# A recurrent cross-attention block with a three-way maxout FFN: transposes moved to DMA, the state read turned round, and the first batch split by halves of heads

## The chip, the cores and the metric

The kernel runs on one core of one Trainium2 chip. The metric is the device time of one execution in microseconds, the lower the better. Three runs of the kernel before gave 189.73, 190.93 and 191.05 us, median 190.93 us. The profile is of one further execution.

## The reference

For each of 8 batches and 8 heads there are 512 tokens x and 32 states, both 64 wide. Tokens attend to states, states attend to tokens, and the 544 rows that result go, with the heads side by side as 512 columns, through a maxout FFN.

```python
B, H, S, Ns, D = 8, 8, 512, 32, 64          # n_tokens 4352, d_model 512, d_ff 768
scores = scale * x @ state^T                 # per batch and head: 512 x 32
a      = softmax(scores, over the states)
xread  = a @ state                           # 512 x 64
a2     = softmax(scale * state @ x^T, over the tokens)
sread  = a2 @ x                              # 32 x 64
y      = concat([xread, sread], rows), heads side by side      # (8*544) x 512
h      = max(max(y @ w1, y @ w2), y @ w3)    # w: 512 x 768
out    = h @ w_out                           # w_out: 768 x 512
```

Both softmaxes come from the same exponentials e = exp(scale * scores), and no maximum is subtracted in the kernel. For the token rows the kernel never forms xread: since xread @ w = a @ (state @ w), it computes G = state @ w for each batch (a row for every head and state, 256 rows by 2304 columns) and multiplies that by the transposed a.

## The kernel before, in words

TensorE (PE) does all products. In the names below, b is a batch, m one of six slices of 128 columns of d_ff, j one of four groups of 128 tokens, h a head.

- `xt_piece` transposes x of a batch on PE, 16 blocks of 128x128, into `pxt`; ScalarE (ACT) copies it out as `xT` (lines 134 and 135).
- `score_piece` makes the scores `ps` from `xT` and `bd`, the transposed states laid out block-diagonally for pairs of token groups. ACT takes the exponential `e`; VectorE (DVE) sums it (`den`) and inverts (`rden`); GpSimd (POOL), for batch 0 DVE, multiplies to `a`.
- `sread_piece` makes sread with x as the stationary and e as the moving operand, 32 matmuls of 32 columns, then 8 matmuls with a tile of ones for the denominators. DVE divides into `ats`, which holds the state rows of all batches, already transposed.
- `at_piece` transposes a on PE (8 blocks, `pat`); DVE copies it out as `aT`.
- `g_piece` makes one sixth of G: 8 small matmuls in 8 tiles of the array (4 column groups by 2 row groups) into `pg`, and an ACT copy of 128x768 (line 208).
- `maxout` makes, for one m, three products `pw` of 512 columns (w1, w2, w3), and takes the maximum: ACT copies the first out (`t`, line 222), DVE takes the two maxima (lines 223 and 224) into `ht`.
- `ffn_out` multiplies `ht` by w_out for two token groups at once into `po` (12 matmuls), ACT copies 128x1024 out (line 251), and SP starts the output DMA.

Each engine works its instructions off in the order in which the program writes them; that order is written out by hand. The loop over b runs `x_maxout(b, m)` for m = 0 to 5, and behind each m come the pieces of the next batch and the output of the batch before: after m = 0 `xt_piece`, after 1 `score_piece`, after 3 `sread_piece`, after 4 `at_piece`, after each m one `g_piece`, and after 2 and 5 (ahead of that `g_piece`) half of `ffn_out(b - 1)`. In the last batch the slots hold `s_maxout`, the maxout of the state rows. Ahead of the loop, batch 0 goes through all pieces in turn.

PSUM has eight banks: the pool "pw" is a ring of four single banks, which only `pw` uses after the start; the pool "two" is two buffers of two banks, for `pxt`, `ps`, `psr`, `pat`, `pg` and `po`. Matmuls that would reuse a buffer wait until its reader is done.

Loads: x of batch 0 in two halves on SP's queue, all states in one DMA on ACT's, and the weights (cut into two halves of d_ff) and the other x on POOL's queue, which converts to bf16 in flight.

Of the kernel before, what the change touches and what calls it, by code (L numbers as in the profile page):

```python
# [15 lines left out]
def kernel(  # L16
# [86 lines left out]
    pt = [pp.tile([128, 8, 128], BF16, tag="pw", bufs=4, name=f"pt{k}") for k in range(2)]
    for t in range(16):
        nc.tensor.transpose(pt[t // 8][:, t % 8, :], st_sb[:, t].rearrange("p c d -> p (c d)"), ident)
    nc.vector.tensor_copy(out=x_sb[0][:, 0:4].rearrange("p h j d -> p h (j d)"), in_=x_f[0])
    nc.scalar.copy(out=x_sb[0][:, 4:8].rearrange("p h j d -> p h (j d)"), in_=x_f[1])  # L109

    def bd_piece(b0, b1):
        for k in range(2):
            for c, copy in enumerate((nc.vector.tensor_copy, nc.scalar.copy)):
                r = slice(64 * c, 64 * c + 64)
                dst = bd[r, b0:b1, :, c, :].rearrange("p b h (g t) -> p (b h) g t", t=16)
                copy(out=dst[:, :, :, 8 * k:8 * k + 8],
                     in_=pt[k][r, :, 16 * b0:16 * b1].rearrange("p t (k g) -> p k g t", g=2))

    bd_piece(0, 1)


    xT, e, a, aT, G, ht = {}, {}, {}, {}, {}, {}

    def xt_piece(b):

        xT[b] = work.tile([128, H, 2, 128], BF16, tag="xT", name="xT")
        pxt = pp.tile([128, H, 2, 128], BF16, tag="two", name="pxt")
        for h in range(H):
# [197 lines left out]
```

## Time and profile before

| | us |
|---|---|
| median of three runs | 190.93 |
| the profiled execution's own time | 189.44 |
| its span, in which the rows below count | 187.6 |
| PE busy | 163.5 (87%) |
| ACT busy | 106.2 (57%) |
| DVE busy | 103.3 (55%) |
| POOL busy | 28.0 (15%) |

The profiled execution is 1.49 us shorter than the median of the runs, and 1.84 us of it lie outside the span. A busy share is an average over the whole span. The span has stages with different limits: a start in which batch 0 goes through its pieces, the loop over the batches, and an end in which only outputs are left. The rows below are read stage by stage. A row of the timeline merges neighbouring instructions of one line; its first number is the start, the second how long the group took.

### The profile page before, as it was taken

How to read it: one execution, taken by the hardware profiler on the slowest of the kernel's cores; microseconds unless marked ns; L12 is line 12 of the kernel's file. 1: busy time of each engine (PE TensorE's matmuls, PEld its weight loads, DVE VectorE, ACT ScalarE, POOL GpSimd, SP SyncE). 2: the span in 40 equal slices, each digit the busy share in tenths (PEclk: the TensorE clock that was granted, in tenths of full speed). 3: DMA queues.
4: the chain of work that ended last, by engine and by line, in shares of the span. 5: the costliest groups of instructions: out<-in, count | busy, mean ns of one | idle time of the engine just before them, and what ended most of it. 6: DMA issues, size and time to landing. Idle time of an engine off the chain costs nothing.

```text
span 187.6 us, 3845 instructions
## 1 busy us (share of the span) xinstructions
PE 163.5 (87%) x1604; PEld 84.8 (45%) x1604; DVE 103.3 (55%) x161; ACT 106.2 (57%) x151; POOL 28.0 (15%) x31
## 2 busy tenths in 40 slices
PE   0643699899999999999999999999999999999990
PEld 0632244454445444544454454445454546565530
DVE  4429325994592559255925683467447747476100
ACT  3542769469455955495549554955495544242330
POOL 8710000500500050005000500040004000000021
PEclk9999999999999999999999999999999999999998
DMA  5999990180192019110911092202020202020236
GB/s 194 265 203 203 203 165 3 6 106 3 77 151 84 31 56 165 68 54 33 182 47 77 9 193 37 103 0 112 5 112 0 115 2 112 3 112 0 112 139 197
DMA packets 15216, 17.53 MB, mean 93 GB/s; under 512 B 672, under 2 KB 12704, under 8 KB 15200
## 3 DMA queue, kind: packets, MB, share of 16 engines
q0 software_dynamic: 11360, 7.08, 27.1%
q1 hardware_dynamic: 3696, 9.70, 13.3%
q10 hardware_dynamic: 144, 0.52, 0.8%
q8 instruction: 12, 0.20, 0.4%
q14 instruction: 4, 0.03, 0.1%
HBM read 15.20 MB, written 8.91 MB: 129 GB/s over the span
## 4 chain that ended last, share of the span: by engine, by line
PE 54%; ACT 18%; DVE 16%; issue 6%; DMA 4%; SPq 0%; DVEq 0%; ACTq 0%
PE pw L218 22%; PE po L243 22%; ACT G L208 7%; PE pg L203 4%; PE pxt L130 4%; DVE rd L176 4%; ACT xT L135 4%; DVE t L223 4%; DMA xf<-in_x_dram 3%; DVE ht L224 3%; ACT xT L134 2%; ACT t L222 2%; ACT osb L251 2%; DVE ats L177 1%; DVE den L148 1%
## 5 line engine op out<-in xcount | busy, mean ns | idle before, releaser
L218 PE MATMUL pw<-aT,G 128*128 128x512 bf16 x288 | 72.0, 384 | 0.7 <-ACT t L222 0.6
L223 DVE TENSOR_TENSOR t<-t,pw 128x512 bf16<-128x512 bf16 (+1 forms) x54 | 34.9, 647 | 55.4 <-ACT t L222 52.1
L208 ACT CAST G<-pg 128x768 bf16<-128x768 f32 x48 | 38.8, 812 | 15.6 <-PE pg L203 15.5
L243 PE MATMUL po<-wout,ht 128*128 128x512 bf16 x204 | 46.5, 379 | 0.0
L218 PEld LDWEIGHTS <-G 128*128 128x128 bf16 x288 | 24.8, 98 | 32.5 <-issue 11.3
L224 DVE TENSOR_TENSOR ht<-t,pw 128x512 bf16<-128x512 bf16 (+1 forms) x54 | 35.5, 658 | 6.0 <-PE pw L218 0.5
L251 ACT COPY osb<-po 128x1024 f32<-128x1024 f32 x16 | 16.2, 1012 | 37.3 <-PE po L243 37.3
L222 ACT CAST t<-pw 128x512 bf16<-128x512 f32 (+1 forms) x54 | 31.4, 584 | 6.9 <-PE pw L218 5.4
L153 POOL TENSOR_TENSOR a<-e,rden 128x1024 bf16<-128x1024 bf16 x7 | 13.3, 1904 | 116.9 <-DVE rden L150 116.9
L243 PEld LDWEIGHTS <-ht 128*128 128x128 bf16 x204 | 19.9, 98 | 23.9
L203 PE MATMUL pg<-w,bd 64*32 64x384 bf16 x384 | 18.1, 353 | 7.2 <-DVE ats L177 6.1
L203 PEld LDWEIGHTS <-bd 64*32 64x32 bf16 x384 | 6.6, 90 | 17.3 <-issue 9.8
L134 ACT COPY xT<-pxt 128x1024 bf16<-128x1024 bf16 x8 | 8.1, 1012 | 5.0 <-PE pxt L130 5.0
L148 DVE TENSOR_REDUCE den<-e 128x32 f32<-128x1024 bf16 x8 | 9.7, 1213 | 2.0 <-ACT e L146 2.0
L130 PE MATMUL pxt<-ident,x 128*128 128x128 bf16 x128 | 9.5, 231 | 0.1
L146 ACT ACTIVATE e<-ps 128x1024 bf16<-128x1024 f32 x8 | 8.5, 1064 | 1.6 <-PE ps L141 1.6
L130 PEld LDWEIGHTS <-x 128*128 128x128 bf16 x128 | 8.5, 104 | 2.0 <-ACT x L109 0.4
L218 PE MATMUL pw<-ats,w 128*128 128x256 bf16 x72 | 9.0, 272 | 0.2 <-ACT t L222 0.2
L141 PE MATMUL ps<-bd,xT 128*128 128x64 bf16 x128 | 5.6, 199 | 3.7 <-ACT xT L135 2.3
L141 PEld LDWEIGHTS <-xT 128*128 128x128 bf16 x128 | 5.1, 101 | 6.9 <-issue 4.3
L218 PEld LDWEIGHTS <-w 128*128 128x128 bf16 x72 | 7.0, 98 | 2.4 <-issue 0.3
L176 DVE RECIPROCAL rd<-psr 128x128 f32<-128x128 f32 x8 | 7.6, 949 | 0.0
(37 smaller groups left out, 78.6 us busy)
## 6 DMA issues: line engine op xcount, KB each, us to landing
out_dram<-osb SPq DMA_DIRECT2D x15, 512.0 KB, 2.6
x<-in_x_dram POOLq DMA_DIRECT2D x7, 512.0 KB, 7.1
w<-in_moe_w_dram POOLq DMA_DIRECT2D x6, 384.0 KB, 10.6
xf<-in_x_dram SPq DMA_DIRECT2D x2, 512.0 KB, 5.9
wout<-in_moe_w_out_dram POOLq DMA_DIRECT2D x1, 768.0 KB, 18.6
stf<-in_state_dram ACTq DMA_DIRECT2D x1, 512.0 KB, 4.1
out_dram<-osb SPq DMA_DIRECT2D x2, 256.0 KB, 3.0
out_dram<-osb SPq DMA_DIRECT2D x4, 64.0 KB, 1.7
```

The costliest lines, as they stand in the source:

```text
L130: nc.tensor.transpose(pxt[:, h, jj, :], x_sb[b][:, h, 2 * jj:2 * jj + 2, :].rearrange("p j d -> p (j d)"), ident)
L134: nc.scalar.copy(out=xT[b][:, 0:4], in_=pxt[:, 0:4])
L153: mul(out=a[b].rearrange("p j h n -> p (j h) n"), in0=e[b].rearrange("p j h n -> p (j h) n"), in1=rden.rearrange("p j h -> p (j h)").unsqu ...
L176: nc.vector.reciprocal(out=rd, in_=psr[:, 128:256])
L203: nc.tensor.matmul(pg[32 * hh:32 * hh + 32, r, 0:384], bd[64 * r:64 * r + 64, b, h, r, :], w_sb[c][64 * r:64 * r + 64, hh, k * 384:(k + 1) ...
L208: nc.scalar.copy(out=G[b][:, :, u * 384:(u + 1) * 384], in_=pg[:, :, 0:384])
L218: nc.tensor.matmul(p[:, 0:n], lhs(i, m, k), rhs(k), start=(k == 0), stop=(k == nk - 1))
L222: nc.scalar.copy(out=t0[:, 0:n], in_=pw[0][:, 0:n])
L223: nc.vector.tensor_max(t1[:, 0:n], t0[:, 0:n], pw[1][:, 0:n])
L224: nc.vector.tensor_max(ht[b][:, m, :], t1[:, 0:n], pw[2][:, 0:n])
L243: nc.tensor.matmul(po[:, j - j0, :], ht[b][:, m, j * 128:(j + 1) * 128], wout_sb[:, m, :], start=(m == 0), stop=(m == NM - 1))
L251: nc.scalar.copy(out=o, in_=po)
```

## The change

The arithmetic is the same up to rounding. The parts:

- **First batch.** x of batch 0 comes in two halves by parity of the head; the states of batch 0 have a small DMA of their own (`st0`) and a tile of their own (`bd0`), the rest (`stf`, `bdr`) comes third on SP's queue. Scores, softmax and transposes of batch 0 run by halves. `x_maxout(0, m)` starts when the first sixth of G is there, and the other sixths are made in between. Batch 1 has its front part behind batch 0, with PE transposes; the loop starts at b = 1.
- **Weights** are loaded in three chunks of d_ff: one slice, two slices, three slices. G is stored by slice of d_ff, and one `g_cols` call makes one or two slices; from batch 1 on they come in pairs.
- **sread** has e as the stationary operand (32 columns wide, four column tiles of the array) and x with a block of ones behind it as the moving operand, 128 columns: the denominators come out of the same 32 matmuls. The result `sr` is not yet transposed.
- **DMA transposes** on SP's queue: `sr` into `ats` for every batch, `x` into `xT` and `a` into `aT` from batch 2 on.
- **po in single banks**: `ffn_out` works on one token group (6 matmuls, one bank of the ring "pw", an ACT copy of 128x512). `psr` uses that ring too.
- **keep_busy** puts five matmuls on zeros at the start of PE's program.

The diff, cut to its core (removed lines are left out except at the loads; they are the functions shown above):

```diff
--- before.py
+++ after.py
...
+    st0_f = data.tile([128, 2, D], F32, name="st0f")
+    nc.scalar.dma_start(out=st0_f, in_=state[0].rearrange("h n d -> (h n) d").rearrange("(t p) d -> p t d", p=128))
+    x0_f = [data.tile([128, HS, J * D], F32, name=f"x0f{g}") for g in range(2)]
+    for g in range(2):
+        nc.sync.dma_start(
+            out=x0_f[g], in_=x[0].rearrange("(s g) (p j) d -> g p s (j d)", g=2, j=J)[g])
     st_f = data.tile([128, 16, D], F32, name="stf")
-    nc.scalar.dma_start(
+    nc.sync.dma_start(
         out=st_f, in_=state.rearrange("b h n d -> (b h n) d").rearrange("(p t) d -> p t d", t=16))
-    x_f = [data.tile([128, 4, J * D], F32, name=f"xf{g}") for g in range(2)]
-    for g in range(2):
-        nc.sync.dma_start(out=x_f[g], in_=x_rows(0)[:, 4 * g:4 * g + 4, :])
+    zero = const.tile([128, 512], BF16, name="zero")
+    nc.vector.memset(zero, 0.0)
     ident = const.tile([128, 128], BF16, name="ident")
     make_identity(nc, ident)
...
+    chunks = ((0, 1), (1, 3), (3, 6))
+    w_sb = [wpool.tile([128, HS, 3, (m1 - m0) * 128], BF16, name=f"w{m0}") for m0, m1 in chunks]
     wout_sb = wpool.tile([128, NM, d_model], BF16, name="wout")
     def load_w(c):
+        m0, m1 = chunks[c]
         for i, w in enumerate((moe_w1, moe_w2, moe_w3)):
             nc.gpsimd.dma_start(
+                out=w_sb[c][:, :, i, :],
+                in_=w.rearrange("(kk p) f -> p kk f", p=128)[:, :, m0 * 128:m1 * 128])
...
     load_w(0)
     load_w(1)
+    bd0 = data.tile([128, H, 2, Ns], BF16, name="bd0")
+    nc.vector.memset(bd0, 0.0)
+    bdr = data.tile([128, B - 1, H, 2, Ns], BF16, name="bdr")
+    for b in range(B):
+        nc.vector.memset(x_sb[b][:, XW:XW + D], 1.0)
+    load_w(2)
     load_x(1)
     nc.gpsimd.dma_start(out=wout_sb, in_=moe_w_out.rearrange("(kk p) f -> p kk f", p=128))
-    ones = const.tile([128, 64], BF16, name="ones")
-    nc.vector.memset(ones, 1.0)
+    nc.gpsimd.memset(bdr, 0.0)
+    load_x(2)
...
+    def keep_busy(n):
+        p = pp.tile([128, 1024], F32, tag="two", name="idle")
+        for _ in range(n):
+            nc.tensor.matmul(p[:, 0:512], zero[:, 0:128], zero, start=True, stop=True)
...
+    def states_first():
+        st0 = data.tile([128, 2, 2, D], BF16, name="st0")
+        nc.vector.tensor_copy(out=st0, in_=st0_f.unsqueeze(2).to_broadcast((128, 2, 2, D)))
+        p = pp.tile([128, 2, 128], BF16, tag="pw", bufs=4, name="pt0")
+        for t in range(2):
+            nc.tensor.transpose(p[:, t, :], st0[:, t].rearrange("p c d -> p (c d)"), ident)
+        for c, copy in enumerate((nc.vector.tensor_copy, nc.scalar.copy)):
+            r = slice(64 * c, 64 * c + 64)
+            copy(out=bd0[r, :, c, :], in_=p[r].rearrange("p t (h n) -> p (t h) n", n=Ns))
...
+    def x_transpose_dma(b):
+        new(xT, b, [128, H, 2, 128], "xT")
+        nc.sync.dma_start_transpose(out=xT[b].rearrange("p h j t -> p (h j) t"), in_=x_sb[b][:, 0:XW])
...
+        if n == 2:
+            p = pp.tile([128, J, n, HS, Ns], F32, tag="two", name="ps")
+        else:
+            p = pp.tile([128, J, n, HS, Ns], F32, tag="pw", bufs=4, name="psh")
...
+    def a_transpose_dma(b):
+        new(aT, b, [128, J, 2, 128], "aT")
+        nc.sync.dma_start_transpose(
+            out=aT[b].rearrange("p j g t -> p (j g) t"), in_=a[b].rearrange("p j g s n -> p (j g s n)"))
+    def sread(b):
+        p = pp.tile([128, 2, 2, D], F32, tag="pw", bufs=4, name="psr")
         for j in range(J):
+            for g in range(2):
+                for s in range(HS):
+                    xj = xv[b][:, 2 * s + g, j, :]
+                    both = bass.AP(xj.tensor, xj.offset,
+                                   (xj.ap[0], (XW - ((2 * s + g) * J + j) * D, 2), (1, D)))
+                    nc.tensor.matmul(
+                        p[32 * s:32 * s + 32, g], e[b][:, j, g, s, :], both,
+                        start=(j == 0 and g == 0), stop=(j == J - 1), skip_group_check=True,
+                        tile_position=(0, 32 * s))
+        rd = work.tile([128, 2, 1], F32, tag="rd", name="rd")
+        nc.vector.reciprocal(out=rd, in_=p[:, :, 1, 0:1])
+        sr = work.tile([128, 2, D], BF16, tag="sr", name="sr")
+        nc.vector.tensor_mul(out=sr, in0=p[:, :, 0, :], in1=rd.to_broadcast((128, 2, D)))
+        nc.sync.dma_start_transpose(
+            out=ats[:, b].rearrange("p s n -> p (s n)"), in_=sr.rearrange("p g d -> p (g d)"))
+    def g_cols(b, ms):
+        for m in ms:
+            if m == 0:
+                new(G, b, [128, 2, NM * 384], "G")
+            w, f = w_cols(m)
+            p = pp.tile([128, 2, 512], F32, tag="two", name="pg")
+            for s in range(HS):
+                for g in range(2):
+                    nc.tensor.matmul(
+                        p[32 * s:32 * s + 32, g, 0:384].rearrange("p (i f) -> p i f", i=3),
+                        bd(b, 2 * s + g)[64 * g:64 * g + 64, g, :], w[64 * g:64 * g + 64, s, :, f],
+                        start=True, stop=True, tile_position=(64 * g, 32 * s))
...
+    def ffn_out(b, j, split=False):
+        if j == 0:
+            osb[b] = work.tile([128, J, d_model], F32, tag="osb", name="osb")
+        p = pp.tile([128, d_model], F32, tag="pw", bufs=4, name="po")
+        for m in range(NM):
+            nc.tensor.matmul(p, ht[b][:, m, j * 128:(j + 1) * 128], wout_sb[:, m, :],
+                             start=(m == 0), stop=(m == NM - 1))
+        o = osb[b]
+        if split:
+            nc.scalar.copy(out=o[:, j, 0:256], in_=p[:, 0:256])
+            nc.vector.tensor_copy(out=o[:, j, 256:512], in_=p[:, 256:512])
         else:
+            nc.scalar.copy(out=o[:, j, :], in_=p)
...
+        j0 = j if b == B - 1 and j >= 2 else j - 1
+        if j == 1 or j == 3 or j0 == j:
+            nc.sync.dma_start(
+                out=out[b * SP:b * SP + S, :].rearrange("(p j) f -> p j f", j=J)[:, j0:j + 1, :],
+                in_=o[:, j0:j + 1, :])
...
+    keep_busy(5)
+    states_first()
+    dve(out=xv[0].rearrange("p (s g) j d -> p g s (j d)", g=2)[:, 0], in_=x0_f[0])
+    act(out=xv[0].rearrange("p (s g) j d -> p g s (j d)", g=2)[:, 1], in_=x0_f[1])
+    x_transpose(0, 0, dve)
+    x_transpose(0, 1, dve)
+    for g in range(2):
+        scores(0, g, g + 1)
+        softmax(0, g, g + 1, nc.vector.tensor_mul)
+    g_cols(0, (0,))
+    a_transpose(0, 0, act)
+    a_transpose(0, 1, dve)
+    x_maxout(0, 0)
+    states_rest()
+    sread(0)
+    g_cols(0, (1, 2))
+    x_maxout(0, 1)
+    x_maxout(0, 2)
+    g_cols(0, (3, 4))
+    x_maxout(0, 3)
+    x_maxout(0, 4)
+    g_cols(0, (5,))
+    x_maxout(0, 5)
+    x_transpose(1, 0, act)
+    x_transpose(1, 1, dve)
+    x_transpose_dma(2)
+    scores(1, 0, 2)
+    softmax(1, 0, 2, nc.vector.tensor_mul)
+    load_x(3)
+    sread(1)
+    g_cols(1, (0, 1))
+    ffn_out(0, 0)
+    g_cols(1, (2, 3))
+    ffn_out(0, 1)
+    a_transpose(1, 0, act)
+    a_transpose(1, 1, dve)
+    g_cols(1, (4, 5))
+    pending = [(0, 2), (0, 3)]
+    for b in range(1, B):
+        n = b + 1
         slots = [[] for _ in range(NM)]
+        if n < B:
+            slots[0].append(lambda: scores(n, 0, 2))
+            slots[0].append(lambda: softmax(n, 0, 2, nc.gpsimd.tensor_mul))
+            slots[1].append(lambda: g_cols(n, (0, 1)))
+            slots[3].append(lambda: sread(n))
+            slots[3].append(lambda: a_transpose_dma(n))
+            slots[4].append(lambda: g_cols(n, (2, 3)))
+            slots[5].append(lambda: g_cols(n, (4, 5)))
+            if n + 1 < B:
+                slots[4].append(lambda: x_transpose_dma(n + 1))
+            if n + 2 < B:
+                slots[1].append(lambda: load_x(n + 2))
         else:
             for m in range(NM):
                 slots[m].append(lambda m=m: s_maxout(m))
+        for m in (1, 2, 4, 5):
+            if pending:
+                slots[m].append(lambda t=pending.pop(0): ffn_out(*t))
...
+        pending += [(b, j) for j in range(J)]
+    ffn_out(B - 1, 0)
+    ffn_out(B - 1, 1)
+    ffn_out("s", 0)
+    ffn_out("s", 1)
+    ffn_out(B - 1, 2)
+    ffn_out(B - 1, 3, split=True)
```

SP's instruction queue, the whole program before: two loads, then only outputs.

```order
L68 DMA xf_82<-in_x_dram 128x4x256
L68 DMA xf_83<-in_x_dram 128x4x256
L258 DMA out_dram<-osb 128x1024 x15
L255 DMA out_dram<-osb 32x512 x4
L258 DMA out_dram<-osb 128x512 x2
```

SP's queue now, from the output of batch 0 to the output of batch 2 (x_90 and x_91 are x of batches 3 and 4).

```order
L297 DMA out_dram<-osb 128x1024 x2
L232 DMA_TRANSPOSE ats<-sr 128x128
L212 DMA_TRANSPOSE aT<-a 128x8x128
L167 DMA_TRANSPOSE xT<-x_90 128x16x128
L297 DMA out_dram<-osb 128x1024
L232 DMA_TRANSPOSE ats<-sr 128x128
L212 DMA_TRANSPOSE aT<-a 128x8x128
L167 DMA_TRANSPOSE xT<-x_91 128x16x128
L297 DMA out_dram<-osb 128x1024 x2
```

Three transposes stand between the outputs in each batch, in the order sr, a, x: the transposes of a and x are issued only after the sr of the same batch is there.

ACT in one batch of the loop before, from the first `t` (m = 0) to the fourth.

```order
L222 CAST t_560<-pw_551 128x512
L134 COPY xT<-pxt 128x1024
L135 COPY xT<-pxt 128x1024
L208 CAST G<-pg 128x2x384
L222 CAST t_605<-pw_596 128x512
L146 ACTIVATE e<-ps 128x1024
L208 CAST G<-pg 128x2x384
L222 CAST t_654<-pw_645 128x512
L251 COPY osb<-po 128x1024
L208 CAST G<-pg 128x2x384
L222 CAST t_694<-pw_685 128x512
```

ACT in one batch of the loop now, from the first `t` to the fifth.

```order
L262 CAST t_836<-pw_827 128x512
L186 ACTIVATE e<-ps 128x1024
L262 CAST t_875<-pw_866 128x512
L248 CAST G<-pg 128x2x384 x2
L288 COPY osb<-po 128x512
L262 CAST t_920<-pw_911 128x512
L288 COPY osb<-po 128x512
L262 CAST t_943<-pw_934 128x512
L262 CAST t_997<-pw_988 128x512
L248 CAST G<-pg 128x2x384 x2
L288 COPY osb<-po 128x512
```

The two copies of xT are gone, the exponential follows the first `t` directly, G comes two at a time, and the output copies are half as wide and twice as many.

## Rows read from the trace of the kernel before

**Rows 1.** Stretches: start:end, length, busy (count) per engine, PEclk, DMA share, GB/s.

```profile
24.04:39.32 15.28, 14.20 (x172) 6.93 (x165) 9.84 (x16) 10.62 (x16) 2.80 (x2) 1.00 0.48 62
39.32:153.55 114.23, 109.85 (x1137) 54.46 (x1129) 68.22 (x104) 72.53 (x102) 14.99 (x10) 1.00 0.30 73
153.55:174.90 21.35, 21.13 (x140) 12.89 (x133) 12.03 (x22) 8.74 (x16) 0.00 (x0) 1.00 0.12 50
174.90:187.60 12.70, 7.94 (x38) 3.41 (x35) 1.69 (x4) 2.95 (x5) 2.07 (x4) 0.94 0.47 165
```

**Rows 2.** Timeline of PE over one batch, b = 3: start, duration, work.

```profile
77.39 1.47 PE L218 MATMUL pw<-aT,G 128*128 128x512 bf16 x6
78.69 1.06 PE L130 MATMUL pxt<-ident,x 128*128 128x128 bf16 x16
79.68 0.36 PE L203 MATMUL pg<-w,bd 64*32 64x384 bf16 x8
79.97 1.47 PE L218 MATMUL pw<-aT,G 128*128 128x512 bf16 x6
81.77 0.63 PE L141 MATMUL ps<-bd,xT 128*128 128x64 bf16 x16 [0.33 <-ACT xT L135]
82.47 0.35 PE L203 MATMUL pg<-w,bd 64*32 64x384 bf16 x8
...
84.11 2.75 PE L243 MATMUL po<-wout,ht 128*128 128x512 bf16 x12
86.79 0.35 PE L203 MATMUL pg<-w,bd 64*32 64x384 bf16 x8
...
88.48 0.68 PE L163 MATMUL psr<-e,x 128*64 128x32 bf16 x32
...
89.33 0.36 PE L203 MATMUL pg<-w,bd 64*32 64x384 bf16 x8
...
90.92 0.61 PE L186 MATMUL pat<-ident,a 128*128 128x128 bf16 x8
91.86 0.36 PE L203 MATMUL pg<-w,bd 64*32 64x384 bf16 x8 [0.33 <-DVE ats L177]
...
96.43 0.39 PE L218 MATMUL pw<-aT,G 128*128 128x512 bf16 x1
```

**Rows 3.** Groups by line and shape: count, busy, mean ns, idle before.

```profile
L208 ACT CAST G<-pg 128x768 bf16<-128x768 f32 x48 | 38.8, 812 | 15.6 <-PE pg L203 15.5
L224 DVE TENSOR_TENSOR ht<-t,pw 128x512 bf16<-128x512 bf16 x48 | 33.0, 688 | 5.4 <-PE pw L218 0.5
...
L222 ACT CAST t<-pw 128x512 bf16<-128x512 f32 x48 | 29.3, 610 | 4.5 <-PE pw L218 4.5
...
L148 DVE TENSOR_REDUCE den<-e 128x32 f32<-128x1024 bf16 x8 | 9.7, 1213 | 2.0 <-ACT e L146 2.0
```

**Rows 4.** DMA: one queue's totals, then issues with KB each and us to landing.

```profile
q0 software_dynamic: 11360, 7.08, 27.1%
...
out_dram<-osb SPq DMA_DIRECT2D x15, 512.0 KB, 2.6
...
out_dram<-osb SPq DMA_DIRECT2D x4, 64.0 KB, 1.7
```

**Rows 5.** The issues of the x load of batch 0 on SP: ns min/median/max.

```profile
L68 SPq DMA_DIRECT2D xf<-in_x_dram x2: 436/464/492, 0.7 to 1.2; - x2
```

**Rows 6.** Timeline of the start, all engines: start, duration, work, idle before.

```profile
7.78 1.04 ACT L109 CAST x<-xf 128x1024 bf16<-128x1024 f32 x1 [1.91 <-DMA xf<-in_x_dram]
...
15.29 1.23 DVE L153 TENSOR_TENSOR a<-e,rden 128x1024 bf16<-128x1024 bf16 x1
16.44 2.07 DVE L116 COPY bd<-pt 64x896 bf16<-64x896 bf16 x2
17.55 1.90 ACT L116 COPY bd<-pt 64x896 bf16<-64x896 bf16 x2 [3.93 <-DVE bd L116]
...
24.04 2.24 PE L218 MATMUL pw<-aT,G 128*128 128x512 bf16 x6
```

More of the change, by code (lines that the diff above doesn't have):

```diff
@@ L105 @@
[L105 to L111, printed above, removed]
+    nc.scalar.activation(out=warm, in_=zero[:, 0:1], func=AF.Exp, scale=1.0)
@@ L112, in bd_piece, with states_rest @@
+    def states_rest():
+        st = data.tile([128, 16, 2, D], BF16, name="st")
+        nc.vector.tensor_copy(out=st[:, :, 0, :], in_=st_f)
+        nc.scalar.copy(out=st[:, :, 1, :], in_=st_f)
         for k in range(2):
+            p = pp.tile([128, 8, 128], BF16, tag="pw", bufs=4, name="pt")
+            for t in range(8):
+                nc.tensor.transpose(p[:, t, :], st[:, 8 * k + t].rearrange("p c d -> p (c d)"), ident)
             for c, copy in enumerate((nc.vector.tensor_copy, nc.scalar.copy)):
@@ L114, in bd_piece @@
                 r = slice(64 * c, 64 * c + 64)
-                dst = bd[r, b0:b1, :, c, :].rearrange("p b h (g t) -> p (b h) g t", t=16)
+                dst = bdr[r, :, :, c, :].rearrange("p b h (q t) -> p (b h) q t", t=16)
                 copy(out=dst[:, :, :, 8 * k:8 * k + 8],
[L117 to L128, printed above, removed]
+                     in_=p[r, :, 16:16 * B].rearrange("p t (k q) -> p k q t", q=2))
@@ L133, in xt_piece @@
[L133 to L149 removed]
+                    p[:, s, jj, :],
@@ L182, in at_piece @@
-    def at_piece(b):
-        pat = pp.tile([128, 2048], BF16, tag="two", name="pat")
-        for q in range(2):
-            for j in range(J):
-                nc.tensor.transpose(
-                    pat[:, q * 512 + j * 128:q * 512 + j * 128 + 128],
-                    a[b][:, j, 4 * q:4 * q + 4, :].rearrange("p h n -> p (h n)"), ident)
-        aT[b] = work.tile([128, 2, J * 128], BF16, tag="aT", bufs=3, name="aT")
-        nc.vector.tensor_copy(out=aT[b].rearrange("p q t -> p (q t)"), in_=pat[:, 0:1024])
@@ L193 @@
[L193 to L208 removed]
+        mul(
+            out=a[b][:, :, g0:g1].rearrange("p j g s n -> p j (g s) n"),
+            in0=e[b][:, :, g0:g1].rearrange("p j g s n -> p j (g s) n"),
+            in1=rden.rearrange("p j g s -> p j (g s)").unsqueeze(3).to_broadcast((128, J, n * HS, Ns)))
@@ L239, in ffn_out @@
-    def ffn_out(b, j0, j1):
-        po = pp.tile([128, 2, d_model], F32, tag="two", name="po")
-        for j in range(j0, j1):
-            for m in range(NM):
-                nc.tensor.matmul(po[:, j - j0, :], ht[b][:, m, j * 128:(j + 1) * 128], wout_sb[:, m, :],
-                                 start=(m == 0), stop=(m == NM - 1))
-        n = j1 - j0
-        o = work.tile([128, 2, d_model], F32, tag="osb", bufs=3, name="osb")
-        if n == 1:
-            nc.scalar.copy(out=o[:, 0, 0:256], in_=po[:, 0, 0:256])
-            nc.vector.tensor_copy(out=o[:, 0, 256:512], in_=po[:, 0, 256:512])
+        w, f = w_cols(m)
```

179 lines of the change are left out of this document (61 added, 118 removed).

## The prediction, made before the changed kernel ran

> **What bounds the kernel now.** I read the stretches first, then PE's timeline over one batch, then the groups by line, the DMA issues and the start. The first product of batch 0's maxout starts at 24.04 us [rows 6]; from there the stretches run to the next batch at 39.32, through six equal batches (114.23 us, so 19.04 each), the last batch with the state rows (21.35) and the end (12.70); together 187.60 [rows 1]. In the six batches PE is busy 109.85 of 114.23 us, and ACT and DVE about 60 to 64% [rows 1]: the loop is bound by PE's list of work, so whatever leaves that list shortens it, and what only moves between ACT and DVE doesn't. The starts of PE's groups show the list of one batch, from 77.39 to 96.43 [rows 2]: a product of three `pw` takes 1.30 (77.39 to 78.69), six of them 7.80; x transposes 0.99 (78.69 to 79.68); scores 0.70 (81.77 to 82.47), ahead of which PE stands 0.50, since the `pw` from 79.97 are issued by 81.27 and the scores start at 81.77, with ACT's copy of xT as releaser; `po` 2.68 (84.11 to 86.79), twice; sread with its ones 0.85 (88.48 to 89.33); transposes of a 0.94 (90.92 to 91.86, of it 0.33 waiting for `ats` to free the buffer); G 0.29 each (79.68 to 79.97), 1.74. The rest, 0.16, is change-over.
>
> **The loop after the change.** From batch 2 on the transposes of x and a are off PE, and with them go the 0.50 and the 0.33: 0.99 + 0.50 + 0.94 = 2.43, leaving 16.61.
>
> sread: 32 matmuls now stream 128 columns each, 4096 in all, in four column tiles. 512 columns take 0.216 us (six such in 1.30 [rows 2]), so one behind the other they would take 1.73, and in four groups side by side 0.43. That tiles do run side by side is seen in G: 8 x 384 columns would take 1.30 in series, and the interval is 0.29. Nearer is the row of the 32 small sread matmuls, 0.68 [rows 2], since 32 weights must still be loaded. I take 0.75 in place of 0.85; ends 0.43 and 1.73.
>
> G by pairs: the same 48 matmuls. A second group needs the tiles of the first; at most that costs another 0.29 a pair, 0.87 a batch. I take nothing. The two buffers that a pair fills are emptied by ACT in 2 x 0.81 [rows 3]; the next pair is 2.64 behind (a `pw` product and six `po`), which covers it by 1.0 us. Where ACT falls behind by more, PE waits at `pg`.
>
> `po` in single banks: the same 24 matmuls, 5.36 us. ACT's four copies of half the size are put at 0.6 like the copy of `t` (0.61 [rows 3]), so ACT has 6 x 0.61 + 6 x 0.81 + 4 x 0.6 + 1.1 for the exponential, 12.0 of 16.7 us; xT's copies are gone. But `po` and sread now stand in the ring of four banks with `pw`. The tightest place is the third bank of m = 1: DVE empties it only after the row sums (1.21 [rows 3]) and their inverse (0.35), which now come right after m = 0. Counted from the batch's start: scores end at 2.0, exponential to 3.3, sums and inverse to 4.9, two maxima of 0.69 [rows 3] to 6.3; PE wants that bank at 2.0 + 1.30 + 0.58 + 1.34 + 0.87 = 6.1. I add 0.2 (ends 0 and 0.5).
>
> So 16.61 - 0.10 + 0.2 = **16.7 us a batch** in place of 19.04.
>
> **The transposes on SP.** SP had only outputs; now sr, a and x of each batch stand between them, and one behind the other. sr is ready about 1.1 us after sread ends (PE's result, the second maximum 0.69, two short divisions). Until PE needs xT of the batch after, 7.9 us of PE work follow sread (three products of 1.30, two pairs of 0.58, two `po` of 1.34, change-over): xT has **6.8 us** from the issue of sr, aT 5.5. No row shows a transpose. The nearest, the 512 KB output on the same queue, lands 2.6 after its issue, 64 KB after 1.7 [rows 4], and an issue takes 0.46 [rows 5]: 3 x 0.46 + 2.6 = 4.0, hidden by 2.8. The other end: x falls into 16 blocks of 128 rows of 256 bytes, 2048 rows; queue q0 moves its small packets in 27.1% x 187.6 x 16 / 11360 = 71.6 ns each [rows 4, 1], so on 16 engines x would take 9.2, a 4.6, sr 0.6, landing at 14.4 + 0.46 + 1.7 = 16.5. I take 4.0, from the row of the same queue. The cover is only as good as that: past 6.8, each us comes back once in each of the five batches 2 to 6. The load of x three batches ahead now goes out behind POOL's multiplication; it has over 16 us, and lands in about 7.
>
> Here a page speaks for and against. The Trainium skill, Advanced Engine Details and Errata, section X-Bar Transpose (TRN2), has transposes as fast as plain DMAs, which would leave the forecast as it is; the same page's section DGE: Hardware vs Software rates the transpose of the hardware queues, SP's among them, as worse than the software one's, which would be the first rival below. No row of this trace decides between them.
>
> **The start.** The second half of x lands at about 7.75 now, since ACT's cast at 7.78 waited for it [rows 6]. Without half a megabyte of states beside it I put 6.5 (ends 5.5 and 7.75). Then in turn: cast 1.04; 8 transposes 1.1; copy 0.7; scores 0.85; half an exponential 0.6; DVE's softmax by halves 1.4 (half of 1.21, 0.35 and 1.23 [rows 3, 6]) and 0.8 behind the first half; transposes back 0.6; copy 0.4: first product at 14.0 in place of 24.04. But that isn't ten us won, since the rest now follows in a row: the product at half pace and its maxima to 16.8; the states' cast to 17.9, transposes to 18.6, DVE's two copies (2.07) and ACT's second after them (0.9) [rows 6] to 21.6; G 1 to 22.4; two products to 25.1; G 3 to 26.3; two products, G 5 and the last product to 31.4; batch 1: transposes 1.0, copy 0.8, scores 0.7, exponential 1.2, sread 0.85, then G, 12 `po` and transposes of a, 5.0: 41.0. The first product of batch 0 took 2.24 for what later takes 1.47 [rows 6, 2]: 512 columns in 0.427, the 1.2 GHz level, though the granted clock of the stretch reads 1.00 [rows 1]; before it PE had worked with gaps. I take that pace until 25 us: +3. Batch 1 starts at **44.0** (40.5 at full pace with x at 5.5, up to 48), with half of batch 0's `po` (2.68) done that at 39.32 was still all to do. The start loses 2.0 net.
>
> The five dummy matmuls would matter if they kept the clock up. The Trainium skill, TensorE: Matmul & The Clock Gate, Part 1, has half rate as the default that activity lifts and idling brings back; by that they lift nothing, as PE then waits for x. The slow row at 24.04, after a start full of gaps, agrees.
>
> **The sum.** 44.0 + (16.7 - 2.7) + 5 x 16.7 + 22.0 + 12.7 = 176.2 against 187.6. The last batch is put 0.65 above 21.35, as `po` delays the ring (0 to 1.3); the end is as before. That is 11.4 less: 178.0 for the profiled execution (189.44). The median of the runs lies 1.5 higher, so I predict **179.5**.
>
> **Rivals.** (1) *Transposes at twice a plain copy*: they land at 8.0, 1.2 late, five times: 185.5. For: nothing in the trace has their small pieces; against: SP's queue is nearly empty. 184 to 193. (2) *Transposes land late enough to make it slower*: sread, then sr, then a, then x stand in one chain on SP, and PE waits for its last link at the scores. It decides from a landing 6.8 + 11.4/5 = 9.1 us after sr's issue; at q0's price, 16.5, it is 9.7 x 5 = 48.5 more, 228. For: one queue, in order, sr first; against: SP's outputs of 512 KB land in 2.6. (3) *Tiles don't run side by side*, so the change doesn't do what it says: sread in series (+0.98) and second groups of pairs at full length (+0.87), six times: +11.1, 190.6. Against: G's 0.29. (4) *The start comes off better*, at 40.5, and sread at 0.43: 179.5 - 3.5 - 1.9 = 174.
>
> **How the numbers follow.** Forecast 0.47 (174.5 to 184), (1) 0.17, (2) 0.17, (3) 0.08, (4) 0.11. About 1% is what a measurement of this kernel can tell: 189.0 to 192.8 is no change. Faster: 0.47 + 0.11 + 0.13 of (1) + 0.01 of (3) = 0.72; the same 0.04 + 0.05 = 0.09; slower 0.17 + 0.02 = 0.19. The range leaves out (2) and a start better still: 171 to 193.
>
> **What would show it.** Right: starts of batches 2 to 6 some 16.7 apart, no wait of the scores for xT, sread in 0.5 to 0.9, first product near 14, batch 1 near 44. Wrong: `ps` or the first `pw` of a batch released by a DMA (1, 2); sread over 1.2 or a pair of G over 0.8 (3); PE waiting for ACT at `pg` or for DVE at `pw`, over 0.5 a batch, which would mean that the ring and not PE sets the pace.

## The result, and the profile after

The changed kernel takes **182.59 us** (median of 4 runs, 180.44 to 183.48) against 190.51 for the kernel before (four runs: the three named ahead and 190.10): ratio 0.955, 95% interval 0.9455 to 0.9644. That is faster by 4.5%, and 3.1 us above the 179.5 predicted. Medians here and below are of all four runs, while the ratios leave out slow runs (183.48 here, one each in runs 1 and 6, and two in run 3, of which one is the profiled execution). Its profiled execution took 182.44, its span is 180.7.

The stretches of the changed kernel, columns as in [rows 1]: to the first product; batch 0 and the preparation of batch 1; batch 1; batches 2 to 6; the last batch; the end; and, once more by itself, one batch (b = 3).

```profile
0.00:13.56 13.56, 7.27 (x55) 4.12 (x56) 6.87 (x21) 5.37 (x8) 12.32 (x18) 1.00 1.12 212
13.56:43.69 30.13, 23.24 (x257) 10.86 (x257) 15.84 (x25) 16.60 (x24) 2.40 (x3) 1.00 0.94 136
43.69:60.67 16.98, 13.47 (x144) 5.77 (x144) 9.96 (x16) 10.98 (x17) 2.80 (x2) 1.00 0.64 125
60.67:147.91 87.24, 81.82 (x770) 34.45 (x781) 50.26 (x80) 54.04 (x84) 12.20 (x8) 0.98 0.60 118
147.91:168.72 20.81, 20.70 (x131) 12.92 (x132) 12.78 (x24) 7.87 (x17) 0.00 (x0) 1.00 0.13 52
168.72:180.70 11.98, 7.88 (x36) 3.41 (x35) 0.42 (x1) 3.88 (x7) 2.07 (x4) 1.00 0.50 176
79.25:96.97 17.72, 16.17 (x154) 6.71 (x157) 10.05 (x16) 10.98 (x17) 2.79 (x2) 1.00 0.77 137
```

Batch 1 begins at 43.69 (44.0 predicted). Then batch 1 takes 16.98 (14.0), batches 2 to 6 take 17.45 each (16.7), the last 20.81 (22.0), the end 11.98 (12.7). So the loop misses by 3.0 + 3.7, and 2.2 come back elsewhere. The 17.45 is a mean: between the starts of their first `pw`, batches 2 to 6 take 18.58, 17.72, 17.67, 16.55 and 16.72. In the single batch PE is busy 16.17 of 17.72 us: the loop is no longer PE's alone. PE's timeline of that batch, which answers to [rows 2], shows where it stands (the last two lines are the start of batch 6):

```profile
79.25 1.47 PE L258 MATMUL pw<-aT,G 128*128 128x512 bf16 x6 [1.00 <-DMA aT<-a]
80.98 0.64 PE L181 MATMUL ps<-bdr,xT 128*128 128x64 bf16 x16 [0.26 <-DMA xT<-x]
81.46 1.46 PE L258 MATMUL pw<-aT,G 128*128 128x512 bf16 x6
82.85 0.52 PE L244 MATMUL pg<-w,bdr 64*32 64x384 bf16 x16
83.30 1.47 PE L281 MATMUL po<-wout,ht 128*128 128x512 bf16 x5
84.60 1.03 PE L258 MATMUL pw<-aT,G 128*128 128x512 bf16 x4
85.84 0.59 PE L258 MATMUL pw<-aT,G 128*128 128x512 bf16 x2 [0.20 <-DVE ht L264]
...
88.95 0.63 PE L224 MATMUL psr<-x,e 128*32 128x128 bf16 x32
89.51 1.48 PE L258 MATMUL pw<-aT,G 128*128 128x512 bf16 x6
...
94.52 1.47 PE L281 MATMUL po<-wout,ht 128*128 128x512 bf16 x6
96.97 1.47 PE L258 MATMUL pw<-aT,G 128*128 128x512 bf16 x6 [0.98 <-DMA aT<-a]
98.64 0.64 PE L181 MATMUL ps<-bdr,xT 128*128 128x64 bf16 x16 [0.20 <-DMA xT<-x]
...
131.19 1.46 PE L258 MATMUL pw<-aT,G 128*128 128x512 bf16 x6
133.07 0.64 PE L181 MATMUL ps<-bdr,xT 128*128 128x64 bf16 x16 [0.42 <-DMA xT<-x]
```

Both signs that the prediction named as wrong are there: the first `pw` and `ps` are released by a DMA. By intervals, `aT` costs 1.15 (94.52 + 1.30 to 96.97), `xT` 0.43 (79.25 + 1.30 to 80.98) and the ring of PSUM banks 0.37 (84.60 + 0.87 to 85.84); the rest of the list is 15.77. SP's own timeline over the same time, in which the second number is how long the issue held the queue:

```profile
88.37 0.33 SPq L297 DMA_DIRECT2D out_dram<-osb  x1
90.78 1.12 SPq L232 DMA_TRANSPOSE ats<-sr  x1
92.01 1.25 SPq L212 DMA_TRANSPOSE aT<-a  x1
93.35 3.26 SPq L167 DMA_TRANSPOSE xT<-x  x1
```

Counted from sr's issue at 90.78, `aT` is there at 96.97, 6.2 later where the prediction gave 5.5 (in this batch PE's list was done 5.04 after the issue), and `xT` at 98.64, 7.86 later where it gave 6.8. For the whole chain the prediction had 4.0. The DMA totals and issues of the changed kernel beside [rows 4]:

```profile
q1 hardware_dynamic: 23936, 15.21, 33.4%
...
out_dram<-osb SPq DMA_DIRECT2D x15, 512.0 KB, 2.9
x<-in_x_dram POOLq DMA_DIRECT2D x7, 512.0 KB, 6.6
...
ats<-sr SPq DMA_TRANSPOSE x8, 4.7
xT<-x SPq DMA_TRANSPOSE x6, 5.1
aT<-a SPq DMA_TRANSPOSE x6, 4.7
```

The load of x three batches ahead, on POOL's queue, is issued at 86.45 in this batch and takes 6.5: it runs until 93. The copies are issued from 90.78 on, and ahead of them on SP's queue stands an output, issued at 88.37 into that load. Such outputs in this batch and in batch 5, where no load of x runs any more (the last is issued at 104.11 and takes 6.6):

```profile
L297 SPq DMA_DIRECT2D out_dram<-osb x1: 332/332/332, 88.4 to 88.4; - x1
DMA to landing us min/median/max: 7.5/7.5/7.5
...
L297 SPq DMA_DIRECT2D out_dram<-osb x1: 332/332/332, 123.7 to 123.7; - x1
DMA to landing us min/median/max: 2.6/2.6/2.6
```

Two theories follow. **Late:** the copies are issued too late, one behind the other. **Shared:** they would be in time, but the x load takes the DMA engines from them, or from the output ahead of them. A third, that transposing itself is dear, can go with either. The changed kernel's own batch 5 already speaks for a share of each: with no load of x, the first `pw` of batch 6, at 131.19, waits for nothing, while the scores at 133.07 still wait for `xT`. The landing of its copy of a, issued at 127.38, where it was 4.9 in the three batches before:

```profile
DMA to landing us min/median/max: 3.2/3.2/3.2
```

### The profile page after: what moved, and what is told of

Same layout as the page of the kernel before. It is cut to its first block, busy times and chain, and to the rows that moved or that the text cites. A ratio compares the mean times of both kernels' runs of the same rounds, so it can differ in the third digit from the quotient of the medians.

```text
span 180.7 us, 3477 instructions
## 1 busy us (share of the span) xinstructions
PE 154.4 (85%) x1388; PEld 71.5 (40%) x1403; DVE 96.1 (53%) x167; ACT 98.7 (55%) x155; POOL 31.8 (18%) x34
## 3 DMA queue, kind: packets, MB, share of 16 engines
q1 hardware_dynamic: 23936, 15.21, 33.4%
## 4 chain that ended last, share of the span: by engine, by line
PE 50%; DMA 18%; DVE 14%; ACT 9%; SPq 4%; issue 3%; DVEq 0%; ACTq 0%
PE pw L258 28%; PE po L281 14%; DMA xT<-x 11%; DVE t L263 4%; DVE den L193 3%; ACT e L186 3%; DVE ht L264 3%; DMA x0f<-in_x_dram 3%; SPq L212 3%; DMA aT<-a 3%; PE ps L181 2%; PE psr L224 2%; ACT t L262 2%; ACT G L248 2%; PE pg L244 1%
## 5 line engine op out<-in xcount | busy, mean ns | idle before, releaser
L258 PE MATMUL pw<-aT,G 128*128 128x512 bf16 x288 | 75.7, 398 | 10.7 <-DMA aT<-a 6.2
L258 PEld LDWEIGHTS <-G 128*128 128x128 bf16 x288 | 27.6, 101 | 47.5 <-issue 9.0
L288 ACT COPY osb<-po 128x512 f32<-128x512 f32 x33 | 19.3, 586 | 22.3 <-PE po L281 21.8
L193 DVE TENSOR_REDUCE den<-e 128x32 f32<-128x1024 bf16 (+1 forms) x9 | 9.9, 1100 | 6.4 <-ACT e L186 6.4
L244 PE MATMUL pg<-w,bdr 64*32 64x384 bf16 x336 | 10.9, 328 | 0.0
L87 POOL DMA_DIRECT2D w<-in_moe_w_dram x9 | 7.5, 856 | 0.6 <-DMA w<-in_moe_w_dram 0.5
L181 PE MATMUL ps<-bdr,xT 128*128 128x64 bf16 x112 | 5.1, 201 | 1.9 <-DMA xT<-x 1.1
L76 POOL DMA_DIRECT2D x<-in_x_dram x7 | 6.4, 928 | 0.0
L224 PE MATMUL psr<-x,e 128*32 128x128 bf16 x256 | 5.5, 232 | 1.1 <-ACT e L186 1.1
L244 PEld LDWEIGHTS <-bdr 64*32 64x32 bf16 x336 | 3.1, 89 | 8.3 <-issue 8.0
```

The lines of the kernel that those rows point to most:

```text
L181: nc.tensor.matmul(p[:, 2 * jj:2 * jj + 2, g - g0, s, :], xT[b][:, h, jj, :], bd(b, h).rearrange("p c n -> p (c n)"), start=(g == g0 and s ...
L193: nc.vector.reduce_sum(out=den, in_=e[b][:, :, g0:g1], axis=AX.X)
L244: nc.tensor.matmul(p[32 * s:32 * s + 32, g, 0:384].rearrange("p (i f) -> p i f", i=3), bd(b, 2 * s + g)[64 * g:64 * g + 64, g, :], w[64 * ...
L258: nc.tensor.matmul(p[:, 0:n], lhs(i, k), rhs(k), start=(k == 0), stop=(k == nk - 1))
L288: nc.scalar.copy(out=o[:, j, :], in_=p)
```

## The experiments

Medians are of 4 runs; each ratio is to the kernel before on the same chip as the run (190.5 to 191.4). "A batch" is the distance between starts of `x_maxout(b, 0)` on PE.

**1. Both copies moved up** (`e1_order`) (171.74; 0.8977, interval 0.8936 to 0.9018).

```diff
+            slots[2].append(lambda: a_transpose_dma(n))
...
             slots[3].append(lambda: sread(n))
-            slots[3].append(lambda: a_transpose_dma(n))
...
-                slots[4].append(lambda: x_transpose_dma(n + 1))
+                slots[0].append(lambda: x_transpose_dma(n + 1))
```

> Same work; SP issues the transpose of x one batch earlier in its list (right behind the scores) and that of a ahead of sread's, so neither stands behind sr. Theory A (the transposes are late because they are queued behind sr, which comes only after sread): no wait of PE for xT or aT, a batch at 15.8 of PE work plus 0.4 for the ring, 16.1 to 16.3 in place of 17.4, and the 3.3 us wait ahead of batch 2 gone: 170 to 173 us. Theory B (the DMA engines are simply full with outputs, loads and 256-byte pieces at that time): the waits stay, only elsewhere, 180 to 184.

As expected from batch 3 on: 16.13 a batch (72.57 to 88.70 and so on), with no wait for a DMA. Ahead of batch 2 a wait of 1.04 for `aT` is left. SP's timeline of this kernel over one batch:

```profile
73.82 3.71 SPq L167 DMA_TRANSPOSE xT<-x  x1
79.40 1.23 SPq L212 DMA_TRANSPOSE aT<-a  x1
81.25 0.40 SPq L297 DMA_DIRECT2D out_dram<-osb  x1
83.66 1.17 SPq L232 DMA_TRANSPOSE ats<-sr  x1
```

The copy of a is issued 9.3 ahead of its use at 88.70 and needs 7.6 in the median here, more than in the changed kernel: nothing got faster, it only has time. Of the 10.9 us between the two profiled spans, 1.89 are not the order's: batch 1 begins at 41.80 against 43.69, since two products in the start ran at full pace in one execution and at half in the other (below). The other 9.0 are waits and their aftermath.

**2. Transposes of x and a back on PE in the loop** (`e2_pe_transposes`) (179.76; 0.9409, 0.935 to 0.9468).

```diff
...
-            slots[3].append(lambda: a_transpose_dma(n))
...
+            slots[5].append(lambda: a_transpose(n, 0, act))
+            slots[5].append(lambda: a_transpose(n, 1, dve))
...
-                slots[4].append(lambda: x_transpose_dma(n + 1))
+                slots[3].append(lambda: x_transpose(n + 1, 0, act))
+                slots[3].append(lambda: x_transpose(n + 1, 1, dve))
```

> Undoes the DMA transposes of x and a in the loop (PE, ACT and DVE do them as for batch 1); sr keeps its DMA. Theory A: PE's list grows from 15.8 by 1.0 for x and 0.6 for a to 17.4, plus 0.4 to 0.8 of waits in the ring: 17.8 to 18.2 a batch in place of 17.4, without the 3.3 us wait and the slow pace behind it: 181 to 185, so as placed the DMA transposes buy next to nothing. Rival (they do buy their 2.4 us): 190 or more.

A little better than expected: 17.46 a batch, what the changed kernel has with its waits (17.45). As placed, the DMA transposes bought nothing; hidden, as in run 1, they are worth 17.46 - 16.13 = 1.33 a batch. Against the 19.04 a batch of the kernel before, the other parts of the change together are worth 1.58 in the loop: the changed kernel's gain in the loop is theirs.

**3. Batch 0 whole and in turn**, as before, in the changed kernel (180.97; 0.9377, 0.9304 to 0.945), and **4. sread as before** in it (181.68; 0.9502, 0.9453 to 0.9552).

```diff
-    for g in range(2):
-        scores(0, g, g + 1)
-        softmax(0, g, g + 1, nc.vector.tensor_mul)
...
+    scores(0, 0, 2)
+    softmax(0, 0, 2, nc.vector.tensor_mul)
     states_rest()
     sread(0)
...
+    g_cols(0, (0, 1, 2))
+    a_transpose(0, 0, act)
+    a_transpose(0, 1, dve)
+    g_cols(0, (3, 4, 5))
...
-    for b in range(1, B):
+    for b in range(B):
...
```

> Undoes the first batch's interleaving: batch 0 goes through scores, softmax and all of G in turn, whole and not by halves, and the loop starts at b = 0 with batch 1's front part in its slots; loads, chunks of W and everything else as changed. If the split start gains (first product ten us earlier): 186 or more. If it loses, as in the sum of the prediction (2 us net): first product near 20 to 22, batch 1 at 35 to 38 with all of batch 0's output still to do, 176 to 181.

```diff
-                    nc.tensor.matmul(
-                        p[32 * s:32 * s + 32, g], e[b][:, j, g, s, :], both,
...
-        nc.sync.dma_start_transpose(
-            out=ats[:, b].rearrange("p s n -> p (s n)"), in_=sr.rearrange("p g d -> p (g d)"))
...
+                nc.tensor.matmul(
+                    p[64 * r:64 * r + 64, s * Ns:s * Ns + Ns], xv[b][:, h, j, :], e[b][:, j, r, s, :],
...
+        nc.vector.tensor_mul(
+            out=ats[:, b].rearrange("p s n -> p (s n)"), in0=p[:, 0:128], in1=rd)
```

> Undoes the turned sread alone: x stationary and e moving, ones apart, ats written by DVE without a DMA; x and a still by DMA transposes. PE has 0.3 more a batch (0.85 against 0.56). Theory A: a's transpose no longer stands behind sr and is issued 3 us earlier, so PE waits for no DMA: 16.4 to 16.6 a batch, 171 to 175. Theory B: waits as now, 183 to 186.

Neither told its question apart, because waits for DMAs sit on top. Run 3's time lies in the range of its second expectation, that the split loses, but not for the reason given: the first product comes at 25.10, not at 20 to 22, the scores at 43.52 wait 3.63 for `xT`, and batches 3 and 4 then take 17.9. Run 4 missed both expectations. Taking sr out of the chain doesn't bring the copies in time (waits of 1.87 for `aT` and 2.37 for `xT` in batch 2, landings of 6.6 and 6.5 in the median; in each of batches 1 to 4 the copy of a is issued 2.4 to 3.7 behind the load of x), while its last batches, without a wait, take 16.41. That speaks for sharing, as no load of x runs beside the copies there. So both questions were asked again on the order of run 1.

**5. Run 1 with batch 0 in turn** (`e5_order_batch0_in_turn`) (170.83; 0.8917, 0.8862 to 0.8973).

> The order of e1_order, but batch 0 whole and in turn ahead of the loop, as in the kernel before; the loop then runs over all eight batches. Theory A, from the sum: the split start puts the first product 10 us earlier and gives it all back, since the states' other batches, the rest of G and batch 1's preparation then stand in a row; in equal terms (half of batch 0's last matmuls, 2.68, taken off) batch 1 begins at 41.0 with the split and at 39.3 without, so 170 to 172 against 171.7. Rival B: the split is worth what its first product shows, some of the 10 us: 174 or more.

The edit of run 3 on run 1. Theory A: nothing is won by the split. In the profiled executions batch 2 begins at 53.93 against 56.56 with the split, with the same `po` done; 1.04 of the difference is a wait for `aT` that is gone. In the medians the two kernels are 0.9 apart, and their intervals overlap.

**6. Run 1 with sread as before** (174.58; 0.9099, 0.9033 to 0.9166), **7. run 1 with G in single groups** (173.31; 0.9082, 0.9015 to 0.9149).

> The order of e1_order with sread as in the kernel before (x stationary, the ones apart, ats written by VectorE, no transposed copy of sr). Theory A: with no wait for a DMA left in the loop, the time follows PE's list: sread 0.85 in place of 0.56, seven times, 1.7 to 2.0 more: 173.4 to 174. Rival B: sr's copy in SP's queue ahead of the output and of x still costs more than the 0.29 on PE: 170 to 171.7, with the wait of 1.04 for aT in batch 2 smaller.

```diff
-            slots[1].append(lambda: g_cols(n, (0, 1)))
-            slots[4].append(lambda: g_cols(n, (2, 3)))
-            slots[5].append(lambda: g_cols(n, (4, 5)))
+            for m in range(NM):
+                slots[m].append(lambda m=m: g_cols(n, (m,)))
```

> The order of e1_order with G one slice per slot (six groups of eight matmuls) in place of three pairs. Theory A: a group by itself takes 0.29 as before and a pair 0.45, so 0.39 more a batch, six times 2.3: 174. Rival B: the pair's gain is lost in the ring (0.20 to 0.37 waited for ht a batch), and ACT's copies come more evenly with single groups: 171 to 172.

Both as theory A in the loop: 16.41 and 16.47 a batch against 16.13, so the turned sread is worth 0.28 and the pairs 0.34 a batch. Run 6's time lies above the 173.4 to 174 expected; its batch 1 begins at 43.57 against 41.80.

**8. The changed kernel with all x loads issued early** (180.49; 0.9429, 0.9362 to 0.9497), and **9. with plain copies for the transposed ones** (175.45; 0.9209, 0.9162 to 0.9256).

```diff
-    load_x(3)
+    for b in range(3, B):
+        load_x(b)
...
-            if n + 2 < B:
-                slots[1].append(lambda: load_x(n + 2))
```

> The changed kernel itself, its transposes where they are, but all loads of x (batches 3 to 7) issued at the place of the first, so that none runs from about 70 us on beside the transposed copies. Theory A: the copies are late because they are issued late and one behind the other: batches stay 17.2 to 17.7 apart, 181 to 183. Rival B: they are late because x's load takes the DMA engines from them: the waits for aT and xT (1.15 and 0.43 a batch) go from batch 4 on, batches of 16.2 there, 176 to 178.

```diff
-        nc.sync.dma_start_transpose(out=xT[b].rearrange("p h j t -> p (h j) t"), in_=x_sb[b][:, 0:XW])
+        nc.sync.dma_start(out=xT[b].rearrange("p h j t -> p (h j t)"), in_=x_sb[b][:, 0:XW])
```

> The changed kernel with its transposed copies of x, a and sr as plain copies of the same tiles at the same places on SP (so the transposition is left out and the values are those of untransposed tiles). This is what the prediction took for their price. Theory A: the waits are the price of transposing (an issue of 1.1 to 3.3 us, a landing at 4.7 to 5.1): a plain copy of 512 KB lands at 2.6 to 2.9 after an issue of 0.4, so no wait for aT or xT is left in the loop, 16.1 to 16.3 a batch, 171 to 173.5. Rival B: the place in the program alone is too late, or x's load takes the DMA engines from any copy: waits of 0.5 or more a batch stay, 176 or more.

Neither expectation of run 8 holds whole. All loads of x have landed by 49 (the last is issued at 20.5, the longest landing is 28.5), before the first of the copies at 54.30. PE waits for `aT` 2.56 ahead of batch 2, 0.62 and 0.22 ahead of batches 3 and 4 and then no more, but for `xT` still 0.4 to 1.0 a batch, and batches stay at 16.7 to 17.7. (For the 0.62 the profile names ACT's copy of an output as releaser; `aT`, issued at 72.17 and landing 4.6 later, ends it at 76.8.) So without the loads some of the lateness goes, and most of it stays: the median falls by 2.1. In run 9, where `aT` and `ats` are copied plainly too, an issue takes only 0.46 to 0.55, and yet waits of 0.24 to 1.85 stay in four of the batches; its time lies between its two expectations. What the copies cost is in the tile views, issue (ns min/median/max, first and last start) and landing. The changed kernel, `aT` and `xT`:

```profile
L212 SPq DMA_TRANSPOSE aT<-a x6: 1248/1248/1262, 56.1 to 144.1; - x6
DMA to landing us min/median/max: 3.1/4.7/4.9
...
L167 SPq DMA_TRANSPOSE xT<-x x6: 1787/3220/3656, 30.1 to 128.7; - x6
DMA to landing us min/median/max: 4.3/5.1/5.3
```

The plain copies of run 9:

```profile
L212 SPq DMA_DIRECT2D aT<-a x6: 541/542/542, 55.1 to 136.9; - x6
DMA to landing us min/median/max: 2.3/3.7/5.4
...
L167 SPq DMA_DIRECT2D xT<-x x6: 473/551/552, 29.9 to 121.4; - x6
DMA to landing us min/median/max: 3.0/4.9/6.0
```

The least of each is a copy beside which no load of x runs: 2.3 and 3.0 plain, 3.1 and 4.3 transposed. In the batches with a load even a plain copy takes up to 5.4 and 6.0.

**10. Only x's copy moved up** (`e11_x_transpose_early`), a's left (179.61; 0.9434, 0.94 to 0.9469).

> The changed kernel with only the transposed copy of x moved (from slot 4 to slot 0, behind the scores); that of a stays in slot 3 behind sr. Theory A: each copy is late for its own place: the wait for xT goes, that for aT stays at about 1 a batch, batches of 17.1 to 17.3, 177 to 179. Rival B: the two share the DMA engines, so without x behind it the copy of a lands earlier too, and both waits go: 171.5 to 173.

Theory A, though its time lies just above the 177 to 179 expected: no wait for `xT` is left, `aT` waits 0.60, 0.92 and 1.06 in batches 3 to 5 and 3.06 in batch 2, though x no longer runs behind it. So it isn't x's copy that makes a's late.

**11. The sums of the softmax behind the maxima of m = 1** (`e12_softmax_behind_m1`), on run 5 (171.24; 0.898, 0.8948 to 0.9012).

```diff
-            slots[0].append(lambda: softmax(n, 0, 2, nc.gpsimd.tensor_mul))
+            slots[1].append(lambda: softmax(n, 0, 2, nc.gpsimd.tensor_mul))
```

> The fastest so far (e5_order_batch0_in_turn, 170.8) with the softmax's sums and division of the next batch behind the maxima of m = 1 in VectorE's order, not behind those of m = 0. Theory A: what is left in the loop is 0.36 a batch at the third bank of m = 2 (0.20 idle, the rest a slower start), released by ht of m = 1 behind the sums; it goes, 0.36 x 6 = 2.2 less: 168.5 to 169. Rival B: the transposed copy of a is issued 2.2 later with it, 7.1 ahead of its use, and its landing takes 7.5: PE waits 0.4 for aT instead, 170 to 172.

Rival B: the ring's wait is gone, and the copy of a, now later, takes it over: 0.30 to 0.77 a batch.

**12. Run 11 with the x load held back until sr is there** (`e13_x_load_behind_sread`) (168.54; 0.8817, 0.8769 to 0.8864).

```diff
     def sread(b):
...
+        if 1 <= b and b + 2 < B:
+            hold = work.tile([128, 1], BF16, tag="hold", name="hold")
+            nc.gpsimd.tensor_copy(out=hold, in_=sr[:, 0, 0:1])
+            load_x(b + 2)
...
-            if n + 2 < B:
-                slots[1].append(lambda: load_x(n + 2))
```

> The kernel e12_softmax_behind_m1 (171.2), with the load of x two batches ahead held back on GpSimd until sr is there (a copy of one column of sr stands ahead of it), so that it starts after the transposed copy of a has been issued and not 2.5 ahead of it. Theory A: the copy of a lands at 7.5 because the load of x takes the DMA engines; without it, it lands at 3.3 to 4.7 as where the loads were out of the loop, the waits of 0.3 to 0.8 a batch for aT go, 15.8 to 16.0 a batch, 168 to 169.5. Rival B: the landing at 7.5 is set by the output and by sr's copy on the same queue: the waits stay, 171 to 172; or the load, now later, holds up the copy of x and SP with it: 173 or more.

Theory A, and the fastest kernel of the study: its whole range, 167.80 to 168.75, lies below every run of run 5 (169.66 to 171.20). Landing of a's copy in run 11:

```profile
DMA to landing us min/median/max: 3.0/7.6/7.9
```

and in run 12, with the five batches 2 to 6 in one stretch below it:

```profile
L212 SPq DMA_TRANSPOSE aT<-a x6: 1232/1238/1252, 46.8 to 126.0; - x6
DMA to landing us min/median/max: 3.0/3.1/4.6
```

```profile
54.12:133.03 78.91, 78.91 (x782) 34.49 (x781) 49.66 (x80) 54.28 (x86) 12.88 (x11) 1.00 0.64 135
```

In run 11 the load of x is issued 0.07 ahead of the copy of a (64.46 and 64.53), in run 12 it is issued 2.1 behind it (65.26 and 63.13). One column of a copy on POOL takes the landing from 7.6 to 3.1. PE is busy 78.91 of 78.91 us, 15.78 a batch: its list alone, which the prediction put at 16.5.

## Why the prediction was right, and which step failed

The direction and the size came out (range 171 to 193). By the sum's own steps:

- **"Hidden by 2.8" failed.** The chain from sr's issue to `xT` was put at 4.0 (three issues of 0.46 and the landing of an output, 2.6) and took 7.86. The runs split the difference. Plain copies with little beside them take 1.21 for the two issues ahead (from sr's to x's in run 9) + 3.0 = 4.2, about the number predicted. Transposing adds 1.36 in the issues ahead (2.57 for 1.21) and 1.3 in the landing (4.3 for 3.0); the x load adds 1.0 (5.3 for 4.3): 7.87. So the landing of rival (1), 8.0 and a chain of twice the length, is what happened, though its reason, dear transposes, gives 2.7 of the 3.7, and its price of 185.5 did not come, since PE's list was shorter than put. Transposed copies were not as fast as plain ones here: the Trainium skill, Advanced Engine Details and Errata, section X-Bar Transpose (TRN2), which has them equal, does not fit these rows.
- **The first to be late was aT, not xT.** The prediction gave `aT` 5.5 and then argued only over `xT`. With no load of x, `aT` takes 1.23 + 3.2 = 4.4 and is hidden, as in batch 5; in the batches with the load it took 6.2. The x load's new place behind POOL's multiplication was looked at only for its own landing, not for whom it takes the DMA engines from. For the copy of a, run 12 shows the effect by one edit. For the time, issuing late weighs more: with the copies issued earlier (run 1) the changed kernel gains 9.0 us besides the start, without the loads (run 8) 2.1, 0.6 of it in the start, and with the load held back on top of the better order (run 12 against 11) the starts of batches 2 and 6 lie 2.25 closer together. In run 11 the load holds up the copy itself, since the output stands behind it on SP's queue. In the changed kernel the output stands ahead, and how much of the copies' delay comes through it was not separated.
- **Batch 1 was not a full batch.** Its two `po` behind sread are missing, which takes 2.7 off the cover of 5.5. In the trace `aT` of batch 2 had 2.5 (sr issued at 54.90, PE's list done at 57.42) and needed 5.8: the 3.25 waited. And behind that wait PE fell to half pace. The changed kernel's stretches of the wait and behind it, and PE's rows there:

```profile
57.42:60.67 3.25, 0.00 (x1) 0.01 (x1) 1.37 (x2) 1.45 (x3) 0.00 (x0) 1.00 1.12 181
60.67:65.48 4.81, 4.81 (x29) 2.22 (x29) 2.26 (x3) 2.09 (x3) 0.00 (x0) 0.65 0.30 67
```

```profile
60.67 1.98 PE L258 MATMUL pw<-aT,G 128*128 128x512 bf16 x6 [3.25 <-DMA aT<-a]
62.44 1.06 PE L181 MATMUL ps<-bdr,xT 128*128 128x64 bf16 x16
63.32 2.23 PE L258 MATMUL pw<-aT,G 128*128 128x512 bf16 x6
```

  The granted clock of the 4.81 us is 0.65: the larger part of them ran at the 1.2 GHz level, the rest at 2.4. In run 1, with 1.04 waited, the same work up to the next pair of G took 3.16 (56.56 to 59.72), at a granted clock of 1.00. The longer wait thus cost 1.65 more behind it.
- **PE's list was better than put:** sread 0.56 (0.75 put), scores 0.48 (0.70), a pair of G 0.45 (0.58), together 0.80, by which the 16.5 become 15.7. Tiles do run side by side; rival (3) is out.
- **The ring:** 0.37, put at 0.2, within its ends, at the place named (DVE's sums ahead of the maxima of m = 1, the third bank of m = 2). Run 11 shows the cause.
- **The start** came to within 0.3, and as a loss: counted as the prediction counts it, 43.69 - 2.68 = 41.0 against 39.32, so 1.7 where 2.0 was put. The 0.3 is partly luck, since the same start ended at 41.80 in run 1. Run 5 agrees that the split wins nothing.
- **The last batch and the end** were put 1.2 and 0.7 too high: the ring's 0.65 didn't appear, and the end was shorter.

Together -0.3 + 3.0 + 3.7 - 1.2 - 0.7 = 4.5 above the sum of 176.2. The median of the runs then lay next to the profiled execution, and not 1.5 above it, which leaves 3.1. The forecast was therefore nearer than its steps, and that is luck: a list too long by 0.7 a batch hid part of the waits.

Open: run 8's wait for `xT` with the loads gone was not taken apart further (the output and sr's copy are still on its queue). No run tried other counts of the dummy matmuls, nor the chunks of the weights or `po` in single banks by themselves, so what these are worth is not shown.

## What to carry to other kernels

When a transpose moves from TensorE to a DMA, price it as a chain: issue time of every copy ahead of it on the queue, its own landing, and what else uses the DMA engines in those microseconds, also ahead of it on the same queue. The first remedy is the order: here the same copies, issued as early as their inputs allow, gave 6% (run 1), and holding back a load that wasn't urgent another 1.6% (run 12). Check the cover of each copy in the shortest batch of the loop, not in the typical one, and don't judge a neighbouring edit (runs 3 and 4) while such waits lie on top of it.
